# Chunked attention and a gated feed-forward block on one core: another order of all steps, with twelve warm-up products

## The chip, the core and the metric

The kernel runs on one NeuronCore of a Trainium2 chip. The metric is the time of one execution on the device in microseconds (us). It was measured three times before the change: 384.4, 385.7 and 385.95, median 385.7 us. A further execution was recorded by the profiler; all views and rows below are of that one.

## What is computed

Attention in chunks of 32 queries, each of which sees 8 memory keys and 56 neighbouring keys, for 4 batches, 8 heads, 768 positions and heads of 64; then a feed-forward block with a gate that mixes positions:

```
scores = q_chunk @ k_full.T / 8 ;  a = softmax(scores) ;  x = a @ v_full
h = gelu(x @ w_in) ;  u, v = halves of h            # w_in 512 x 1024
v_n = layernorm(v) * g_ln
gated = u * (w_sg @ v_n + b_sg)                      # w_sg 768 x 768
out = x + gated @ w_out                              # w_out 512 x 512
```

All of it is in f32. The large products are made in TensorE's rounded f32 type: each operand is split into a high and a low part, and a product is the sum of high-low, low-high and high-high.

## The kernel before, in words

The work is cut into named **steps**, each of which issues its instructions on one engine. A string `ORDER` (lines 36 to 95) lists all steps by name, and the last loop (lines 577 to 582) issues them in that order. The wrapper `InOrder` (lines 98 to 107) keeps each engine, and the queue of loads on SyncE (SP), in exactly this order; a step waits for the data and for the buffers it needs. A star behind a name picks the second engine that a step may use. So the order is written out by hand for five engines at once, and it is the only thing that says when a buffer is taken and given back.

**Attention** is done in 24 units u (4 batches of 6 blocks of 128 positions). `q`u, `k`u, `v`u are loads on SP (256, 368 and 512 KB). `S`u are the scores on TensorE: 32 small f32 products of two passes each, which makes 64 weight loads and 64 products. `mx`u, `sb`u (maximum and subtraction, VectorE), `ex`u (exponential, ScalarE), `sm`u, `sr`u (sum and reciprocal, VectorE), `nm`u (division, on VectorE, or on GpSimd with a star), `T`u (four transposes on TensorE, units 0 to 9), `p`u (copy from PSUM) and `A`u (attention times values, 64 small products, 64 weight loads) follow. `xc`u copies the result, `xh`u and `xl`u make its high and low part. There is one buffer for the scores, so S of the next unit waits for `sb`; one for A's result, so the next A waits for `xc`; one for the divided exponentials, so the next `nm` waits for `T`; and two each for q and k, so `q2` waits until S0 has run, `k4` until S2 has, and whatever stands behind a waiting load in the SP queue waits too.

**Weights** come as 64-bit floats and are converted on the chip. For each of eight 512 KB pieces of w_in (`ri10` to `ri13` for the half that makes v, `ri00` to `ri03` for the one that makes u) there are `d1` to `d4` (ScalarE and VectorE), `d5` (high part, ScalarE) and `d6` (low part, GpSimd, or VectorE with a star). `g..`, `ga..`, `gb..` load w_sg and split it, `ro.`, `d.o.` are w_out, `cb` and `cbh` load and halve g_ln and b_sg.

**Feed-forward.** `V`bt makes v of one block of 128 positions: 12 products of 512 columns. For the first three blocks of batch 0 it is made in two halves of 256 columns, `Va` with the pieces i10 and i11 and `Vb` with i12 and i13. `v1` to `v9` are gelu, layernorm and the split. `U`, `W` and `O` with three digits make u (12 products of 384 columns), the mixing over positions (18) and the output (12); `u.`, `w.`, `o1` stand behind them, and `out` stores.

A step `zz`n issues n **warm-up products** (line 573): the 128x128 identity times itself into a free PSUM buffer, read by nobody.

```
def warm(n):
    for _ in range(n if mms.free else 0):
        tensor.matmul(mms.free[0][:, 0:P], ident, ident, start=True, stop=True)

for name in ORDER.split():
    if name[0] == "z" and name[1] == "z":
        warm(int(name[2:]))
        continue
    does, eng = steps.pop(name.rstrip("*"))
    does(eng[name.endswith("*")])
```

Of the kernel before, what the change touches and what calls it, by code (L numbers as in the profile page):

```python
# [46 lines left out]
ex7 ga51 v303 T5 p5 sr6 nm6* v403 v503 S8 A5 T6 U000 ga20 v802 mx8 gb51 gb41 gb20 k9 ro0 g30 g01 ga01 xh5 v7
q10 q9 g31 v902* vx03 gb01 p6 xl5 v104 u1003 xc5 vy03 v603 sb8 v204 u2003 sm7 sr7 u1000 u2000 nm7 V05 ex8
u3003 ga31 v304 u4003 v703 v404 v803 S9 sm8 v504 vx04 sr8 mx9 v903 A6 T7 xc6 p7 v105 ga30 v205 u3000 g50 q11
k10 v8 k11 ga50 v305 sb9 u4000 vy04 gb31 gb30 v405 v505 gb50* vx05 nm8* v604 U012 U011 g00 S10 k12 A7 u1012  # L50
u2012 u3012 vy05 v605 mx10 v705 v704 T8 ex9 xc7 p8 U010 U013 v804 u4012 v904* v805 ga00 v905* sb10 A8 S11
d2o0* d3o0 gb00 d1o0 u1010 ro1 sm9 u1011 d4o0 u2011 ex10 xc8 u2010 u3010 u4010 u3011 u4011 d1o1 W003 d2o1 mx11
d3o1 w1003 sm10 d4o1 w2003 d5o1 w3003 d5o0 sr9 nm9* d6o1 ro2 q12 W000 W001 d1o2 d2o2* w1000 w4003* w1001 w2000
d3o2 w2001 sb11 W002 ro3 k13 q13 v11 v9 W011 T9 S12 k14 q14 w1002 w2002 d6o0* W010 w3001 d1o3 p9 d4o2 d2o3
d3o3 d4o3 sr10 d5o3 d6o3* w3000 w3002 u1013 W012 d5o2 mx12 nm10 sb12 w1010 yt10 w2010 ex12 w3010 ex11 w4001
w4000 d6o2 w4002 w1012 S13 mx13 z12 sm12 w2012 A9 z11 sm11 w1011 w2011 w3012 sr11 nm11 yt11 O000 O003 sb13
o1003 O001 u2013 u3013 sr12 o1001 v12 k15 v10 S14 O002 mx14 W013 nm12 ex13 w3011 xh6 xh8 w4012 sb14 u4013 xh7
xl8 V12 w1013 w2013 v112 w3013 o1002 o1000 ex14 w4013* Ed5 Ea5 k16 q15 Ec5 q16 Eb5 out003 S15 out001 out002
out000 k17 w4011* xl7 sm14 v212 yt12 sr14 sm13 V11 v312 sr13 v111 v211 v311 w4010 xl6 O011 U101 nm13* mx15
v411 sb15 v412 v512 yt13 vx12 xc9 A10 u1101 xc10 S16 vy12 v612 v511 A11 ex15 sm15 o1011 vx11 vy11 v611 v711*  # L60
nm14* v712 v812 v912* V10 mx16 U103 v110 v210 v310 u1103 U102 sr15 u2101 v410 sb16 ex16 sm16 u3101 sr16 u4101
v510 u1102 O012 v811 vx10 o1012 q17 S17 mx17 k18 q18 Ea6 Ec6 Eb6 Ed6 out011 O013 O010 u2102 xc11 u3102 xh9
v911 vy10 v610 yt14 o1013 nm15 sb17 u2103 xl9* A12 S18 V13 yt15 v710* v810 xh10 xh11 u4102 xl11 o1010 u3103
v113 xl10 v213 v313 v413 v14 out012 v13 out010 out013 k19 q19 q20 k20 V15 U110 u1110 v513 vx13 u4103 v910 mx18
nm16 sb18 vy13 v613 v713* U113 V14 xc12 v115 v215 v315 u2110 v813 ex17 u1113 v913 A13 S19 v114 v415 v515 vx15
u2113 u3113 v214 v314 v414 v514 vx14 u4113 vy15 z17 v615 v715* U100 U112 U111 u1100 v815 ex18 vy14 v614 v714
u3110 v814 u4110 u1111 v914* u2100 u2111 u3111 u4111 v915 W111 w1111 w2111 sm17 Ed7 W103 w1103 w2103 mx19 W101
w1101 sr17 w3111 w4111 xc13 w3103 u3100 v15 Eb7 Ec7 v16 Ea7 yt16 nm17* W100 A14 w2101 sb19 S20 w3101 u1112
xc14 u2112 u3112 ex19 u4100 w1100 w2100 A15 W102 W110 w1102 w2102 W113 w1110 w1113 w3100 w3102 w2110 w2113
yt17 w4103 W112 w4100 w4102 z18 w4101 w1112 w3110 w3113 O100 w4110* O103 sm18 sr18 u4112 w2112 w3112 o1103  # L70
o1100 O101 o1101 w4112* O102 xh12 xh13 w4113* O111 o1102 nm18 xl12* o1111 O110 sm19 V20 v120 v220 xh14 v320
mx20 sb20 v420 xl13 Ea8 q21 k21 Ed8 out101 Ec8 out103 out111 Eb8 k22 out100 out102 V21 v520 vx20 sr19 yt18
O113 O112 ex20 v121 xc15 vy20 v620 xl14 v221 nm19 A16 xc16 v321 o1110 v421 v521 v720* o1112 xh16 xh15 v820 S21
U202 U201 u1202 o1113 vx21 u2202 mx21 xl15 sb21 vy21 v621 V23 v920 yt19 u3202 v123 v223 u4202 xl16 v721* v323
u1201 v821 ex21 u2201 v423 v523 u3201 v921* vx23 U200 V22 v19 k23 out110 v17 out113 q22 A17 S22 Ec9 Ed9 q23
v18 out112 Eb9 Ea9 v122 xc17 xh17 vy23 v623 v723 v823 v923 v222 v322 xl17* u4201 V24 v422 v522 sm20 vx22 v124
v224 v324 sr20 v424 vy22 v622 V25 U203 v722 v822 v922 v524 u1200 u2200 u3200 u4200 u1203 u2203 v125 U213 v225
vx24 v325 v425 v525 vx25 mx22 U210 vy24 v624 u3203 u1213 u1210 nm20* sb22 v724 v824 U212 A18 xc18 sm21 u4203
u2213 u2210 vy25 S23 A19 U211 v625 u1212 u3213 u2212 sr21 v725 xc19 v825 u3212 u3210 v924 u4213 v925* u4212
yt20 mx23 nm21* yt21 Ea10 v20 Eb10 v21 Ed10 Ec10 W201 W212 w1201 u4210 w1212 w2201 w2212 W210 W200 sb23 w1200  # L80
w2200 w3201 w4201* w1210 w2210 W202 w3200 w3212 w3210 W203 w4210 ex23 ex22 sm22 z23 sr22 sm23 u1211 w1202 sr23
w1203 w2202 w3202 w4202* u2211 w4200 W213 w2203 w3203 w4203 nm22* u3211 u4211 yt22 W211 w1213 w2213 w1211 O203
o1203 O202 w2211 w3213 w3211 w4213 w4211* nm23* A20 O200 xc20 A21 O201 xh18 xh20 w4212* o1200 o1202 yt23 o1201
O213 O212 xh19 xl19 xl20 V31 v131 o1213 out202 out201 Ea11 out200 V32 v132 v232 v332 o1212 v231 v432 v532 Eb11
v22 Ed11 out203 O210 v23 Ec11 out212 v331 v431 xl18 U302 V30 O211 u1302 u2302 vx32 vy32 v632 v732 o1210 out210
v832 xc21 A22 u3302 xc22 v531 vx31 vy31 o1211 v631 v731 U301 xh22 u4302 v831 xh21 v932 v130 v230 A23 xl22 xl21
v931* v330 xc23 xh23 v430 v530 vx30 xl23 V34 V33 U303 v134 u1301 u2301 v234 u3301 v334 vy30 v630 v730 v434
v830 v930 u4301 u1303 v534 vx34 vy34 u2303 v634 v133 u3303 v233 v734 v333 v834 v433 v533 v934 vx33 u4303 V35
U312 v135 v235 v335 v435 v535 U310 u1310 u2310 vx35 u1312 u2312 vy33 v633 v733* v833 u3312 u4312 U313 u1313
u3310 vy35 v635 U311 U300 u4310 v735 v835 v933* v935* W310 u2313 u3313 u4313 W313 w1310 w2310 w1313 w2313 W301  # L90
w1301 w2301 w3301 W303 w1303 w2303 w3310 w3303 W312 W311 w3313 w1312 w2312 w4313* w4301 w1311 u1311 u1300
# [554 lines left out]
```

## Time and profile before

| | |
|---|---|
| median of three runs | 385.7 us (384.4 to 385.95) |
| the profiled execution | 383.29 us |
| its span, first to last instruction | 381.5 us |
| mean granted TensorE clock over the span | 0.998 |
| TensorE (PE) busy | 363.9 us, 95% |
| VectorE (DVE), ScalarE (ACT), GpSimd (POOL) busy | 65%, 41%, 34% |

The rows give, for each instruction or group, the start in us from the span's start, the length, the engine, the line of the code, the operation and the tiles that it writes and reads. PE is TensorE's products, PEld its weight loads. As every instruction is issued through one helper, all have line 106: the tiles tell them apart (`s` scores, `av` attention times values, `mma` to `mmd` the four PSUM buffers of all other products, `na` the divided exponentials, `pair` and `x` the attention's result, `raw`, `m`, `ex` the weights in conversion). An f32 product leaves two records. The column of the granted clock holds the level from the first recorded change on, so that it reads 1.00 also where none had been recorded yet.

### The profile page before, as it was taken

The page shows a single profiled execution, that of the slowest core. Times are in us where ns is not written, and L with a number is a line of the kernel's source. Part 1 is how long each engine was busy: PE and PEld are TensorE (multiplying, and loading weights), DVE is VectorE, ACT ScalarE, POOL GpSimd, SP SyncE. Part 2 cuts the span into 40 slices and gives each one's busy share as a digit, 9 for nine tenths or more (in the row PEclk, how much of TensorE's full clock was granted, in tenths as well). Part 3 has the DMA queues.
Part 4 walks back from the last instruction along what each step waited for, and adds up shares of the span by engine and source line. Part 5 has one row for each costly group of instructions (what it writes and reads, how often), then busy time and mean ns, then how long its engine had stood idle before and what let it go on. Part 6 is the DMA issues. An engine that isn't in the chain of part 4 may idle for free.

```text
span 381.5 us, 11092 instructions
## 1 busy us (share of the span) xinstructions
PE 363.9 (95%) x4788; PEld 340.7 (89%) x4788; DVE 247.5 (65%) x460; ACT 155.3 (41%) x296; POOL 131.3 (34%) x152
## 2 busy tenths in 40 slices
...
GB/s 242 350 316 308 309 181 212 225 66 171 207 173 163 159 74 211 130 95 74 4 11 140 117 217 14 144 10 140 25 3 54 189 50 2 3 0 2 0 63 147
DMA packets 24530, 47.66 MB, mean 125 GB/s; under 512 B 4384, under 2 KB 13600, under 8 KB 24480
## 3 DMA queue, kind: packets, MB, share of 16 engines
...
q8 instruction: 38, 0.62, 0.7%
q14 instruction: 12, 0.10, 0.1%
HBM read 36.96 MB, written 6.29 MB: 113 GB/s over the span
## 4 chain that ended last, share of the span: by engine, by line
PE 94%; DMA 3%; issue 1%; DVE 1%; SPq 0%; POOL 0%; POOLq 0%
PE mmd L106 23%; PE mmc L106 22%; PE mmb L106 19%; PE mma L106 17%; PE av L106 7%; PE s L106 5%; DMA qb<-in_qs 2%; DMA ka<-in_ks 1%; SPq L106 0%; POOL na L106 0%; DVE ea L106 0%; DVE mxa L106 0%; DVE xb L106 0%; POOLq L106 0%
## 5 line engine op out<-in xcount | busy, mean ns | idle before, releaser
L106 PE MATMUL s<-ka,qa 64*32 64x64 f32 x768 | 11.0, 238 | 6.2 <-DMA ka<-in_ks 4.2
L106 PEld LDWEIGHTS s<-ka,qa 64*32 64x32 f32 x768 | 8.9, 112 | 7.9 <-issue 5.1
L106 DVE SCALAR_TENSOR_TENSOR mmc<-mmc,g_half,b_half 128x384 f32<-128x384 f32 x10 | 6.2, 623 | 12.4 <-PE mmc L106 12.4
L106 DVE SCALAR_TENSOR_TENSOR mmd<-mmd,g_half,b_half 128x384 f32<-128x384 f32 x12 | 7.4, 620 | 10.2 <-PE mmd L106 10.2
L106 DVE SCALAR_TENSOR_TENSOR gb<-gb,mmb 128x512 f32<-128x512 f32 x10 | 6.9, 686 | 9.3 <-ACT gb L106 9.3
L106 PE MATMUL s<-kb,qb 64*32 64x64 f32 x768 | 11.0, 238 | 1.7 <-DVE ea L106 1.5
L106 ACT ACTIVATE ea<-ea 128x512 f32<-128x512 f32 x12 | 7.6, 635 | 11.0 <-DVE ea L106 11.0
L106 DVE STREAM_TRANSPOSE y<-na 128x512 f32<-128x512 f32 x14 | 9.8, 702 | 3.4 <-POOL na L106 1.7
L106 PEld LDWEIGHTS s<-kb,qb 64*32 64x32 f32 x768 | 8.9, 112 | 3.5 <-DVE ea L106 1.8
L106 PEld LDWEIGHTS av<-pt,va 64*64 64x64 f32 x512 | 9.3, 145 | 2.9 <-ACT pt L106 1.7
L106 PE MATMUL av<-pt,va 64*64 64x32 f32 x512 | 10.2, 230 | 1.3 <-ACT pt L106 1.3
L106 PE MATMUL mmc<-w_in_hi,paira 128*128 128x512 f32 (+1 forms) x40 | 9.5, 359 | 1.8 <-issue 1.8
L106 DVE TENSOR_REDUCE mxa<-s 128x8 f32<-128x512 f32 x8 | 5.4, 679 | 8.5 <-PE s L106 8.5
L106 PEld LDWEIGHTS av<-pt,vb 64*64 64x64 f32 x512 | 9.2, 145 | 1.9 <-issue 1.1
L106 POOL TENSOR_TENSOR na<-eb,rda 128x512 f32<-128x512 f32 x3 | 3.5, 1169 | 20.2 <-DVE rda L106 16.4
L106 DVE SCALAR_TENSOR_TENSOR ga<-ga,mmb 128x512 f32<-128x512 f32 x6 | 4.1, 681 | 9.8 <-ACT ga L106 9.8
L106 POOL TENSOR_TENSOR pairb<-uf,pairb 128x384 fp32r<-128x384 f32 x3 | 3.0, 1016 | 20.9 <-ACT pairb L106 20.9
L106 PE MATMUL av<-pt,vb 64*64 64x32 f32 x512 | 10.2, 230 | 0.0
L106 DVE SCALAR_TENSOR_TENSOR mmb<-mmb,g_half,b_half 128x384 f32<-128x384 f32 x6 | 3.7, 617 | 9.9 <-PE mmb L106 9.9
L106 POOL TENSOR_TENSOR paira<-uc,paira 128x384 fp32r<-128x384 f32 x3 | 3.1, 1047 | 20.1 <-ACT paira L106 20.1
L106 ACT ACTIVATE ga<-ga 128x512 f32<-128x512 f32 x12 | 7.6, 632 | 6.0 <-DVE ga L106 5.9
L106 PEld LDWEIGHTS av<-pt,vc 64*64 64x64 f32 x512 | 8.4, 135 | 1.8 <-issue 1.3
...
## 6 DMA issues: line engine op xcount, KB each, us to landing
...
va<-in_vs SPq DMA_DIRECT2D x8, 512.0 KB, 5.4
vb<-in_vs SPq DMA_DIRECT2D x8, 512.0 KB, 4.8
vc<-in_vs SPq DMA_DIRECT2D x8, 512.0 KB, 4.6
pt<-y SPq DMA_DIRECT2D x112, 32.0 KB, 1.9
...
```

Source lines behind the costliest of these rows:

```text
L106: return self.tc.keep_in_program_order(getattr(self.engine, name)(*args, **kw))
```

## The change

`ORDER` is replaced as a whole; nothing else is touched. The same steps stand in another order, some on their other engine, and the warm-up products become twelve instead of four: six ahead of S0, five between T1 and T2, one behind T4 (before: three ahead of S0 and one behind Vb02). The first lines of both strings, which hold the stretch that the prediction works out, and the last ones:

```
-zz1 q1 q0 k0 k1 ri11 ri10 zz2 S0 mx0 sb0 ex0 z0 sm0 sr0 q2 k2 S1 mx1 sb1 S2 d2i11* d2i10* ex1 d3i11 d3i10 sm1
-d1i10 d4i10 sr1 v0 ri13 k3 q3 ri12 v1 nm0* d5i10 T0 p0 nm1* A0 mx2 sb2 ex2 sm2 d1i11 d2i13* d1i13 d4i11 d3i13
-sr2 d4i13 d6i10 S3 T1 nm2* T2 xh0 d5i11 xl0 d6i11 xc0 d5i13 p1* A1 d2i12* d1i12 mx3 sb3 d3i12 d6i13* d4i12 xc1
-ex3 sm3 p2 xh1 xl1* v2 d5i12 d6i12* q5 ri00 d2i00* d1i00 ri01 Va00 A2 Vb00 d2i01* d1i01 d3i00 d4i00 d3i01 sr3
-d4i01 d5i00 v100 xh2 v200 v300 q4 ri02 k4 xl2 cb ri03 v3 k5 Va01 S4 q6 k6 g21 g41 g20 g40 g11 nm3* Vb01 T3
-d5i01 d2i02* xc2 v101 p3 d2i03* d1i02 Va02 v400 v500 mx4 vx00 d3i02 cbh v201 sb4 vy00 v600 v700 v800 v900
-d3i03 d4i02 A3 S5 Vb02 mx5 sb5 zz1 S6 ex4 xc3 xh3 sm4 xl3 V03 v301 v401 sr4 v501 d1i03 v102 v202 d4i03 d5i03
-d5i02 v302 ex5 d6i00* nm4 d6i02* d6i01 q7 g10 v6 v4 k7 v5 U001 T4 vx01 vy01 z5 v601 d6i03* ga40 gb40 v402 mx6
...
-out302 out303 out312 O301 o1301 out301 out213 O300 o1300 out300 O311 o1311 out311
+zz4 zz1 q0 q1 zz1 k0 k1 S0 mx0 sb0 ex0 z0 S1 sm0 sr0 nm0* ri12 ri13 mx1 sb1 T0 q2 k2 v0 q3 k3 ri10 d2i12*
+d2i13* d1i12 d1i13 d3i12 d3i13 d4i12 d4i13 p0 ex1 d5i12 d5i13 S2 mx2 sb2 ex2 d6i13 A0 xh0 d2i10* sm1 sr1 S3
+sm2 xl0 mx3 sr2 nm1* d6i12 T1 nm2* d3i10 sb3 k4 ri11 d1i10 p1 d4i10 d2i11* d1i11 d5i10 ri01 q4 ri00 d2i01* xc0
+v1 d3i11 d4i11 d5i11 ex3 zz1 zz4 T2 Vb00 S4 p2 d2i00* d1i01 d1i00 A1 xc1 xh1 v2 ri02 d2i02* k6 cb q5 k5 v3
+ri03 g40 g10 q6 g21 d6i11 d3i01 d6i10* sm3 sr3 nm3 d3i00 d4i01 d4i00 d5i01 T3 Va00 A2 v100 xl1 mx4 d3i02 sb4
+v200 Vb01 Va01 xh2 xl2 ex4 v300 v400 sm4 sr4 d5i00 d1i02 v101 xc2 p3 v500 v201 d4i02 d6i00* vx00 d6i01 cbh
+nm4* Vb02 S5 A3 T4 vy00 v600 mx5 sb5 v700 d1i03 xc3 d2i03* v301 zz1 v800 d3i03 d4i03 xh3 d5i02 ex5 p4 z5 v900*
+xl3* U001 Va02 S6 V03 d6i02 v401 v501 sm5 v102 v202 sr5 vx01 d5i03 d6i03 u1001 q7 ga21 v302 ga10 mx6 sb6 ex6
...
+out212 out311 out300 O312 O301 o1301 o1312 o1302 out312 O303 out301 out302 o1303 out303 O310 o1310 out310
```

TensorE's own steps up to the first full V product are, before: S0 S1 S2 T0 A0 S3 T1 T2 A1 Va00 A2 Vb00 Va01 S4 Vb01 T3 Va02 A3 S5 Vb02 zz1 S6 V03 (then U001 T4). After: S0 S1 T0 S2 A0 S3 T1 zz1 zz4 T2 Vb00 S4 A1 T3 Va00 A2 Vb01 Va01 Vb02 S5 A3 T4 zz1 U001 Va02 S6 V03.

## Rows read from the trace of the kernel before

**Rows 1.** The page of the profile, parts 1 and 4: busy time of the engines over the span, and the shares of the chain of work that ended last.
```profile
PE 363.9 (95%) x4788; PEld 340.7 (89%) x4788; DVE 247.5 (65%) x460; ACT 155.3 (41%) x296; POOL 131.3 (34%) x152
...
PE 94%; DMA 3%; issue 1%; DVE 1%; SPq 0%; POOL 0%; POOLq 0%
```

**Rows 2.** The view by windows, the first 40 us in stretches of ten: start and end, length, busy us (and instructions) of PE, PEld, DVE, ACT and POOL, the granted clock column, the share of the DMA engines in use and the GB/s that they moved.
```profile
0.00:10.00 10.00, 2.87 (x76) 2.36 (x80) 1.38 (x2) 1.35 (x2) 0.80 (x9) 1.00 0.70 245
...
10.00:20.00 10.00, 6.56 (x261) 5.48 (x262) 8.21 (x16) 6.99 (x13) 3.52 (x4) 1.00 0.97 358
...
20.00:30.00 10.00, 8.67 (x154) 7.61 (x155) 8.23 (x13) 7.27 (x14) 2.28 (x2) 1.00 0.86 285
...
30.00:40.00 10.00, 9.51 (x248) 8.93 (x247) 9.83 (x19) 8.98 (x18) 6.88 (x7) 1.00 0.96 331
```

**Rows 3.** The view of the waits, TensorE alone, over the whole span: who waited for whom, us in total, times, longest.
```profile
PE s L106 <- DMA ka<-in_ks: 4.2, 1, 4.2
...
PE mmc L106 <- issue: 1.8, 1, 1.8
```

**Rows 4.** The timeline of the first 30 us, TensorE's products alone: start, us, engine, line, operation, out<-in, shapes, count. In order: three warm-up products (two records each), the transpose step T2, the value step A1, four 256-column products of Va00, the value step A2, four 256-column products of Vb00.
```profile
1.42 1.65 PE L106 MATMUL mma<-ident 128*128 128x128 f32 x6 [1.42 <-POOL mhalf L106]
...
22.29 1.12 PE L106 MATMUL mmc<-ident,na 128*128 128x128 f32 x4 [1.33 <-POOL na L106]
...
23.33 1.93 PE L106 MATMUL av<-pt,vb 64*64 64x32 f32 x64
...
27.07 1.05 PE L106 MATMUL mmd<-w_in_hi,paira 128*128 128x256 f32 x4
...
28.05 1.20 PE L106 MATMUL av<-pt,vc 64*64 64x32 f32 x64
...
29.77 0.63 PE L106 MATMUL mmd<-w_in_lo,paira 128*128 128x256 f32 x4
```

**Rows 5.** The chain of work that ended last, in order of time (start, us, what, records): the first load of keys, S0, a half V product, a warm-up product, T4, a U product right behind a score step, a V product, an S step, an A step, a W product, an O product, and the addition behind the last O product.
```profile
1.62 5.51 DMA ka<-in_ks
...
7.28 1.19 PE s L106 x61
...
30.87 1.41 PE mma L106 x12
...
41.97 0.22 PE mmb L106 x2
...
48.08 0.44 PE mma L106 x4
...
52.45 2.30 PE mma L106 x12
...
54.75 2.78 PE mmd L106 x12
...
57.97 0.79 PE s L106 x53
...
58.76 1.06 PE av L106 x64
...
354.74 3.12 PE mmd L106 x18
...
371.39 2.08 PE mmd L106 x12
...
377.67 0.56 DVE xb L106
```

**Rows 6.** Instruction loading. First part 3 of the page, the row of the queue that brings instructions (packets, MB, share of 16 engines); then the DMA view of three short stretches, 14.3 to 14.4, 39.0 to 39.1 and 45.75 to 45.85 us, in each of which one packet of that queue began; then the timeline of TensorE from the value step A3 on (the idle time before a row and what ended it stand in brackets).
```profile
q8 instruction: 38, 0.62, 0.7%
...
q8 instruction: 1, 0.02, 58.8%
...
q8 instruction: 1, 0.02, 60.4%
...
q8 instruction: 1, 0.02, 67.2%
...
36.45 1.14 PE L106 MATMUL av<-pt,va 64*64 64x32 f32 x64
...
37.51 0.86 PE L106 MATMUL s<-kb,qb 64*32 64x64 f32 x64
...
38.87 0.63 PE L106 MATMUL mmc<-w_in_lo,paira 128*128 128x256 f32 x4
...
41.34 0.63 PE L106 MATMUL mmc<-w_in_hi,paira 128*128 128x256 f32 x4 [1.83 <-issue]
```

**Rows 7.** The timeline of the first 23 us, the other engines: the maximum of unit 0, GpSimd's division for unit 0, the maximum of unit 2, and a low part of a weight on GpSimd.
```profile
8.49 0.69 DVE L106 TENSOR_REDUCE mxa<-s 128x8 f32<-128x512 f32 x1 [8.49 <-PE s L106]
...
11.94 1.04 POOL L106 TENSOR_TENSOR na<-ea,rda 128x512 f32<-128x512 f32 x1 [1.12 <-DVE rda L106]
...
15.50 0.64 DVE L106 TENSOR_REDUCE mxc<-s 128x8 f32<-128x512 f32 x1
...
16.76 1.27 POOL L106 TENSOR_TENSOR w_in_lo<-ma,w_in_hi 128x512 fp32r<-128x512 f32 x1
```

**Rows 8.** The load of unit 1's values: its issue in the timeline, and its row in the DMA view of 12.65 to 13.2 us, whose last number is the us from issue to landing.
```profile
12.71 0.46 SPq L106 DMA_DIRECT2D vb<-in_vs  x1
...
vb<-in_vs SPq DMA_DIRECT2D x1, 512.0 KB, 8.4
```

More of the change, by code (lines that the diff above doesn't have):

```diff
@@ L42 @@
-d5i01 d2i02* xc2 v101 p3 d2i03* d1i02 Va02 v400 v500 mx4 vx00 d3i02 cbh v201 sb4 vy00 v600 v700 v800 v900
-d3i03 d4i02 A3 S5 Vb02 mx5 sb5 zz1 S6 ex4 xc3 xh3 sm4 xl3 V03 v301 v401 sr4 v501 d1i03 v102 v202 d4i03 d5i03
-d5i02 v302 ex5 d6i00* nm4 d6i02* d6i01 q7 g10 v6 v4 k7 v5 U001 T4 vx01 vy01 z5 v601 d6i03* ga40 gb40 v402 mx6
-sm5 v701 sb6 u1001 ga11 p4 ga21 ga10 U002 v801 A4 S7 U003 v502 u1002 sr5 u2002 vx02 u2001 ex6 xh4 u3001 xl4
-v901* xc4 v103 u3002 ga41 gb21 gb11 nm5* vy02 z6 v602 gb10 v702* u4001 mx7 sm6 sb7 V04 g51 k8 q8 u4002 v203
@@ L47 @@
[L47 to L91, printed above, removed]
@@ L92 @@
-w3312 u2311 u3311 u4311 w2311 w3311 W300 W302 w4311* w4303* w4312* u2300 u3300 w1300 u4300 w2300 w1302 w2302
-w3302 w4310 O312 o1312 O310 O313 w4302* w3300 w4300 O302 o1313 o1310 out310 out313 out211 O303 o1303 o1302
-out302 out303 out312 O301 o1301 out301 out213 O300 o1300 out300 O311 o1311 out311
+zz4 zz1 q0 q1 zz1 k0 k1 S0 mx0 sb0 ex0 z0 S1 sm0 sr0 nm0* ri12 ri13 mx1 sb1 T0 q2 k2 v0 q3 k3 ri10 d2i12*
+d2i13* d1i12 d1i13 d3i12 d3i13 d4i12 d4i13 p0 ex1 d5i12 d5i13 S2 mx2 sb2 ex2 d6i13 A0 xh0 d2i10* sm1 sr1 S3
@@ new lines @@
+xl3* U001 Va02 S6 V03 d6i02 v401 v501 sm5 v102 v202 sr5 vx01 d5i03 d6i03 u1001 q7 ga21 v302 ga10 mx6 sb6 ex6
+g20 k7 vy01 v601 nm5* u2001 v402 v4 ro0 v5 k8 A4 v701 u3001 ga20 xh4 v801 S7 T5 ga40 p5 z6 mx7 xl4 v502 vx02
+u4001 sm6 gb20 sr6 U002 sb7 v901 gb10 gb21 vy02 g11 xc4 ga11 u1002 v103 v203 u2002 v303 u3002 u4002 gb40* v403
+k9 v503 v602 v702 vx03 nm6* g01 q8 gb11 v6 g51 g31 q9 v7 g41 g30 V04 U003 A5 ex7 ga51 gb51* vy03 v603 S8 T6
+xh5 p6 ga01 ga41 v802 sm7 xl5 u1003 xc5 v703 mx8 u2003 gb01 sb8 sr7 u3003 v803 v902 U000 V05 v104 S9 A6 v903
@@ new lines @@
+gb41 u4003 v204 nm7* ex8 ga30 sm8 v105 sr8 v205 ga31 v304 v404 v305 v405 v505 g50 k10 q10 k11 q11 v8 v9 U012
+T7 mx9 u1000 v504 vx04 sb9 ga50 p7 xc6 gb50 u1012 u2000 u3000 d2o0* nm8* gb31 u4000 u2012 u3012 g00 U011 A7
+S10 vy04 v604 v704 vx05 mx10 u4012 vy05 v605 v705* gb30* sb10 U010 xc7 u1010 v804 T8 U013 p8* ga00 v805 v904*
+gb00* v905* d3o0 d1o0 u1011 u2010 u3010 u4010 ex9 A8 S11 u2011 mx11 u3011 u4011 d4o0 sm9 sr9 k12 ro1 W003
+d2o1* d1o1 ex10 w1003 w2003 w3003 d5o0 d3o1 W000 w1000 nm9 sb11 w2000 ex11 w3000 w4000 d4o1 d5o1 d6o1 z11
@@ new lines @@
+w4003 d6o0 W001 sm10 w1001 w2001 xc8 w3001 q12 ro2 d2o2* sr10 w4001* d3o2 k13 q13 d1o2 ro3 v11 W002 T9 w1002
+w2002 p9* w3002 S12 mx12 d4o2 nm10 sm11 d2o3* u1013 d1o3 d5o2 W012 sb12 d3o3 d4o3 d5o3 ex12 u2013 w1012 w2012
+yt10 W011 sr11 w1011 w2011 d6o3 d6o2* S13 nm11* w4002* A9 W010 u3013 w3011 k14 k15 q14 q15 O003 yt11 z12 sm12
+u4013 sr12 w4011* nm12 Ea5 mx13 sb13 o1003 O001 O000 O002 xh8 w3012 xh7 xh6 ex13 S14 o1000 W013 o1001 o1002
+xl6* xl7* w1010 mx14 w4012* sb14 Ed5 Ec5 Eb5 yt12 w2010 out003 v10 xl8 V12 v112 w3010 S15 V11 U101 q16 w1013
@@ new lines @@
+v12 k16 out002 out001 q17 k17 out000 v212 mx15 w4010* w2013 w3013 w4013 O011 ex14 v312 xc9 A10 sm13 sr13 v412
+v512 vx12 vy12 nm13 sb15 v111 ex15 xc10 S16 sm14 sr14 yt13 nm14* v612 o1011 A11 V10 u1101 v211 mx16 v712 v812
+v912* v311 sb16 v411 v110 xc11 v210 u2101 v310 v410 v510 v511 vx11 U102 O012 o1012 O013 O010 xh11 S17 vy11
+v611 xh10 vx10 o1013 sm15 sr15 v711 v811 vy10 v610 v710 xh9 U103 q18 Ed6 k18 Ec6 Ea6 Eb6 A12 mx17 yt14 nm15
+sb17 u1102 u2102 o1010 ex16 ex17 u3102 u1103 u2103 u3103 u3101 v810 yt15 S18 xl11 xl9 V13 xl10 v911 u4102 sm16
@@ new lines @@
+sr16 V15 nm16* u4101 mx18 v113 v213 v313 v910* sb18 k19 q19 v15 out011 v13 v14 out012 out013 out010 v413 v513
+vx13 vy13 v613 u4103 v713 ex18 v115 v813 v913 v215 v315 v415 v515 vx15 V14 U110 u1110 u2110 xc12 v114 v214
+v314 u3110 U113 u1113 A13 S19 v414 vy15 z17 v615 v715 v514 vx14 u2113 vy14 v815 xc13 u3113 u4113 mx19 U100
+u1100 u2100 v915 v614 U111 U112 v714 v814 u4110 sm17 v914* u1111 u3100 u4100 W100 w1100 Ed7 Ec7 Eb7 q20 v16
+Ea7 w2100 w3100 W101 yt16 sr17 nm17 sb19 u2111 u3111 u4111 W111 w1101 w2101 yt17 w1111 w2111 W103 k20 A14
@@ new lines @@
+w3111 xc14 w1103 w2103 w3103 w4103 S20 A15 W113 W102 u1112 u2112 u3112 w1113 w2113 w1102 mx20 w2102 W110 w1110
+w2110 W112 w1112 u4112 w4111 w4100 w3113 w3101 w4101 w3102 w4102 z18 sm18 w2112 O102 O100 O101 w3112 ex19
+w3110 O103 o1102 w4110 w4113* sr18 o1101 o1100 o1103 nm18* w4112 O110 sb20 o1110 O113 xh13 xl13 xh14 xh12 xl12
+V20 v120 v220 v320 ex20 O112 V21 Eb8 Ea8 Ec8 Ed8 yt18 v420 v520 sm19 out103 q21 vx20 v121 v221 sr19 xl14 o1113
+O111 vy20 v620 v720* out101 v17 out100 k21 k22 out102 v321 xc15 v421 S21 A16 xh15 v820 xl15 nm19 v521 U202 V23
@@ new lines @@
+v920* vx21 vy21 v621 xc16 u1202 v721 v821 xh16 v123 v921 o1111 o1112 u2202 v223 V22 U201 out113 v18 q22 out112
+k23 v19 mx21 u3202 u4202 v323 yt19 sm20 v423 v122 U200 v523 vx23 sr20 A17 vy23 xl16 v623 v723* v222 v322 sb21
+v422 u1200 u2200 u3200 ex21 v522 vx22 u1201 v823 xc17 S22 V24 xh17 v923* Eb9 out111 q23 Ec9 Ea9 v20 Ed9 out110
+U203 u4200 u2201 u3201 v124 v224 v324 vy22 v622 xl17 v722 mx22 v822 V25 v424 v922* v524 nm20* u1203 v125 u4201
+vx24 vy24 v225 v325 v624 v724* v425 U213 U210 v525 vx25 vy25 v625 v725* u2203 u3203 u1213 u2213 u1210 v824
```

15 lines of the change are left out of this document (added).

## The prediction, made before the changed kernel was run

> **What bounds the kernel now.** I read the page first: TensorE holds 95% of the span and 94% of the chain that ended last [rows 1]. Then the chain in order of time, for the price of each step at the high clock [rows 5]: S 0.79, A 1.06, T 0.44, half V 1.41, V 2.78, U and O 2.08, W 3.12 us, a warm-up product 0.22, and 0.22 more for a product right behind an S or an A (2.30 against 2.08). With the counts of the program (64 U and O, 32 W, 21 V and 6 halves, 24 S and A, 10 T, 23 such changes, one warm-up product behind S0) the work from S0 on is 353.9 us. S0 starts at 7.28, when its keys have landed, and the last product ends at 377.67 [rows 5]; so 16.5 us are lost. Where: by the end of Va00, at 28.05 [rows 4], the work done was worth 8.2 us of 20.8, which leaves 12.5; one wait of 1.83 inside Vb02 [rows 3, 6]; the rest is spread in tenths. So only the first 42 us can give anything: the other 336 us run without a wait of TensorE.
>
> Two things make up the 12.5. TensorE waits for a chain over the other engines. And it runs at the lower of its two clocks, 1.2 GHz: the column of the granted clock shows 1.00 here [rows 2], but durations don't. T2 took 1.12, A1 1.93, four 256-column products 1.05 at 27.07; then A2 took 1.20 and four such products 0.63 at 29.77 [rows 4]. The clock rose at about 28.1. TensorE had not been idle since 22.29 [rows 4], 5.8 us earlier.
>
> **The change, first stretch.** I walk the new order with these durations. Up to S1 nothing differs: k0 is the third load in both orders, S0 starts at 7.28, and the six warm-up products ahead of it (0.55 each at the low clock [rows 4]) end by 4.7, in time that is idle anyway [rows 3]; cost nothing. The division nm0 ends at 12.98 [rows 7]. T0 now goes before S2: 13.05 to 14.2, its copy p0 to 14.8; S2 14.2 to 15.4, so mx2 begins at 15.5, exactly as before [rows 7]. A0 can start at 15.4 instead of 16.66; I add 0.8 for an instruction packet (below), so it ends at 18.1, S3 at 19.3. T1 needs nm1 (ready 19.0): 19.3 to 20.4. Five warm-up products at 0.55: to 23.15. T2's input is ready at 21.6 (nm2 behind T1, 1.04 on GpSimd), so they delay it by 1.5 us; that is their price, up to 24.25 for the end of T2. Vb00 is then ready (low parts on GpSimd at 1.27 each [rows 7] done at 20.3, xl0 at 19.5).
>
> **When the clock rises** decides the next term. From T1 at 19.3 TensorE would not be idle again; with the 5.8 us of before the clock rises at 25.1. Bounds: 19 to 21, if the stretch from T0 to S3 already suffices, and 28.1, as before. I take 25.1, as it is the same interval in the same kind of work. The TensorE page of the Trainium skill (TensorE: Matmul & The Clock Gate, Part 1) speaks against such a search: the moment differs between runs of one kernel, and one should not fit to it. By that rule part of what a single profile shows here would not come back in the next run; one profile of before cannot show it.
>
> From there: Vb00 to 26.3, S4 27.1, A1 27.2 to 28.3, T3 28.75, Va00 30.3, A2 31.4, Vb01 33.0, Va01 34.4, Vb02 35.8, S5 36.6, A3 37.7, T4 38.15, one warm-up product, U001 40.4, Va02 41.85, S6 42.65, V03 45.6. The same set of steps was done before at the end of T4, 48.52 [rows 5]: a gain of **2.9 us**. What is left after it is the same set of steps in both, with 20 instead of 18 product-behind-S-or-A changes and no T behind an A instead of three (0.15 each): equal. The end is the same too: the last O, an addition of 0.56 [rows 5] and a store.
>
> **What must stay hidden for that.** Loads: v1 now stands behind ri11, ri01, q4 and ri00, and k4 holds SP from 12.6 until S2 has run. About 6.03 MB had moved by 20 us [rows 2]; v1 ends 7.39 MB in the new queue, so 1.36 MB more at 358 GB/s is 23.8, and 2.0 for the lag that the old v1 shows (5.70 MB, moved at 19.1, landed 21.1 [rows 8]): 25.8 against 27.2. At 285 GB/s [rows 2] it is 26.8, still in time. q5, k5 and v3 now wait behind k6 and so for S4 (27.1): v3 ends 1.93 MB later, at 331 GB/s [rows 2] 32.9 and the lag, 34.9 against 36.6. VectorE is busy 9.83 of 10 us between 30 and 40 [rows 2], and nm3 moves to it (0.69); in my walk its products come 0.6 to 1.5 us ahead of their use (xl1 30.8 for Vb01 at 31.4, xl2 32.9 for Vb02, d6i00 37.0 for U001, xl3 41.5 for V03 at 42.65). A slip there of 1 us is inside the range.
>
> **The instruction wait.** In 38 packets of 16 KB [rows 6] the 9576 loads and products [rows 1] come some 252 to a packet. Before, TensorE stood still for 1.83 us although nothing was awaited, in front of its 1462nd instruction (counted from the program: 128 for an S or A, 8 for a T, 24 for a half V), and went on 2.3 us after a packet had begun at 39.05 [rows 6]. A packet is thus asked for about 252 instructions ahead: at number 1209, in A3, 36.6 [rows 6], which makes 4.7 us from request to use. A3 and S5 hold 256 instructions and take under 2 us, so the packet came late. In the new order S5 and A3 are neighbours again: number 1209 is in Vb02 (34.9), number 1461 near the end of A3 (37.6). That is 2.7 us against 4.7: a wait of 2.0. At best the sequencer asks while it is still some products ahead of the array, and the wait is nothing. I take the middle, **1.0 us** back. For the same reason A0 gets its 0.8 (first packet at 14.3 to 14.4 [rows 6], plus 2.3, less the 15.9 at which its 452nd instruction is due). The Trainium skill's page on the launch (Runtime: NRT & Kernel Launch, Instruction fetch mechanics) calls the crossing of a packet mostly hidden; by it the term would be zero, which the 1.83 contradicts here at least once.
>
> **Sum.** -2.9 + 1.0 = -1.9 us. The profiled execution (383.29 for a span of 381.5) lies 2.4 below the median; I put the difference on the median: 385.7 - 1.9 = **383.8 us**. A measurement of this kernel can tell about 0.5% from no change, 1.9 us: the forecast lies on that bound.
>
> **Rivals.** (a) No instruction wait in A3 and none elsewhere: 385.7 - 2.9 = 382.8. For it: 37 of 38 packets cost nothing before. Against: S5 and A3 stand together again under loaded DMA engines. (b) An early rise of the clock, at 19 to 21: the warm-up products shrink to 0.22, T2 ends near 22.4, Vb00 to Va00 1.5 us sooner: 382.3, and 381.3 together with (a). Against: before, the stretch from 16.66 to 20.95 with one gap of 0.15 did not raise it. (c) The clock rises no earlier than before, at 28.1: Vb00 and S4 stay low, 1.0 us is lost: 384.8, no difference that can be told. (d) Slower: instruction packets bound the denser order. The packet of 45.8 came 4.4 us after the request at 41.34, so request to use can be 6.7. In the new order the packets at number 957 (in A1, 4.8 us after the one before) and 1461 (2.7) then wait 1.9 and 4.0: 5.9 lost against 2.9 won, 388.7. It turns into a loss from 5.2 us on ((5.2 - 4.8) + (5.2 - 2.7) = 2.9). Against: the only late packet measured took 4.7.
>
> **Chances and range.** Forecast 0.35 (half of it beyond the bound), (a) 0.20, (b) 0.12, (c) 0.20, (d) 0.13. Faster by over 0.5%: 0.17 + 0.20 + 0.10 = 0.47; within: 0.18 + 0.02 + 0.18 + 0.03 = 0.41; slower: 0.02 + 0.10 = 0.12. Range 381.3, (a) with (b), to 386.4, which leaves out the worse half of (d). The likeliest case's own range is 382.8 to 384.8.
>
> **What would show it.** S0 at 7.3, T0 near 13.1, T1 near 19.3, Vb00's first products near 24.3; the first A of about 1.1 instead of 1.93 tells when the clock rose (A1 by the forecast). A wait by nothing inside A3, 0 to 2 us, near 37. V03 ending near 46.6. After that no wait of TensorE above a few tenths. It is wrong if Vb00 starts after 25.5, if A1, A2 or A3 waits for a load, or if the steps behind V03 hold waits that sum to over 1 us.

## The result, and the profile of the changed kernel

| | before | changed |
|---|---|---|
| median of 21 runs of each | 384.42 us (382.25 to 388.9) | 388.0 us (383.72 to 390.68) |
| ratio of the times, 95% interval | | 1.0075 [1.0047, 1.0104] |
| the profiled execution, and its span | 383.29, 381.5 us | 386.5, 384.4 us |

The ratios, here and below, leave out slow runs, those more than 1.5% above the fastest of their kernel.

The change made the kernel slower. The prediction was 383.8 us in a range of 381.3 to 386.4: the sign is wrong and the range misses the median. It was counted from the 385.7 us of three runs; 21 runs put the kernel before at 384.42, and from there the forecast gain of 1.9 us leads to 382.5. In the two profiled executions the last product ends 3.4 us later than before (the addition behind it starts at 381.06 instead of 377.67 [rows 5]), so the profile holds most of the loss. It must be looked for twice: in the first stretch, which the prediction walked, and behind it, which the prediction put at nothing.

**The first stretch.** The view by windows, two stretches of ten us (columns as in [rows 2]):

```profile
0.00:10.00 10.00, 4.51 (x108) 4.00 (x109) 1.38 (x2) 1.71 (x2) 0.81 (x9) 1.00 0.75 247
...
20.00:30.00 10.00, 9.68 (x197) 9.24 (x199) 9.46 (x17) 8.95 (x16) 4.30 (x4) 1.00 1.01 343
```

In the first ten us the six warm-up products and an S0 0.37 earlier show (4.51 busy instead of 2.87 [rows 2]), in time that is idle otherwise. Between 20 and 30 us TensorE is busy 9.68 instead of 8.67 [rows 2] and does 197 instead of 154 products: there the new order wins. The timeline of its products in the same stretch, in the form of [rows 4]: S0, T0, A0, T1, five warm-up products, T2, the three parts of Vb00, A1, S5, A3 and the three parts of V03:

```profile
6.91 1.17 PE L106 MATMUL s<-ka,qa 64*32 64x64 f32 x64 [2.56 <-DMA ka<-in_ks]
...
12.67 1.12 PE L106 MATMUL mma<-ident,na 128*128 128x128 f32 x4 [1.90 <-POOL na L106]
...
15.94 1.93 PE L106 MATMUL av<-pt,va 64*64 64x32 f32 x64
...
19.49 1.11 PE L106 MATMUL mmb<-ident,na 128*128 128x128 f32 x4 [0.51 <-POOL na L106]
20.40 2.34 PE L106 MATMUL mmc<-ident 128*128 128x128 f32 x10
22.54 1.06 PE L106 MATMUL mmc<-ident,na 128*128 128x128 f32 x4
23.25 1.20 PE L106 MATMUL mmd<-w_in_hi,paira 128*128 128x256 f32 x4
24.24 0.76 PE L106 MATMUL mmd<-w_in_lo,paira 128*128 128x256 f32 x4
24.84 0.63 PE L106 MATMUL mmd<-w_in_hi,paira 128*128 128x256 f32 x4
...
26.57 1.14 PE L106 MATMUL av<-pt,vb 64*64 64x32 f32 x64 [0.32 <-ACT exe L106]
...
35.10 0.86 PE L106 MATMUL s<-kb,qb 64*32 64x64 f32 x64
36.92 1.14 PE L106 MATMUL av<-pt,va 64*64 64x32 f32 x64 [0.96 <-DMA va<-in_vs]
...
43.08 1.20 PE L106 MATMUL mmd<-w_in_hi,pairb 128*128 128x512 f32 x4
44.12 1.09 PE L106 MATMUL mmd<-w_in_lo,pairb 128*128 128x512 f32 x4
45.05 1.10 PE L106 MATMUL mmd<-w_in_hi,pairb 128*128 128x512 f32 x4
```

The length tells the clock: four 256-column products take 1.20, then 0.76, then 0.63, so it rose inside Vb00, near 24.5, and A1 takes 1.14 where it took 1.93 before [rows 4]. V03's successor starts at 46.08; the same set of steps ended at 48.52 before (T4 in [rows 5]). The first stretch gained 2.4 us in this execution. A3 did wait, not for instructions but for v3's load.

**Behind V03.** The view of the waits, TensorE alone (columns as in [rows 3]):

```profile
PE s L106 <- DMA ka<-in_ks: 3.5, 2, 2.6
PE mmb L106 <- DVE ua L106: 2.9, 1, 2.9
PE mma L106 <- POOL na L106: 1.9, 1, 1.9
PE av L106 <- ACT xa L106: 1.5, 1, 1.5
```

The second and the fourth row are new; they lie at 181 and 128 us, where TensorE had no wait before. The chain of work that ended last, near 120 us (start, us, what), shows the one at 128:

```profile
118.85 0.80 PE s L106 x53
...
120.06 0.69 SPq L106
...
120.79 6.80 DMA out<-xa
...
127.70 0.59 ACT xa L106
...
128.34 1.29 PE av L106 x63
```

SP's queue holds the two loads q17 and k17 ahead of out000, the store of a finished block. q17 is released by S15, which ends at 119.65; so the store is issued at 120.79, and it lands 6.8 us later (the two stores ahead of the loads, issued at 117.2 and 117.6, took 6.7 and 8.0). Only then may ScalarE write the same buffer (xc9), only then is A9's result out of `av`, and A10, which writes `av` next, stands for 1.53 us. The wait at 181 has a longer root. The changed kernel's SP queue, VectorE and TensorE there, three timelines one behind the other:

```profile
161.63 8.12 SPq L106 DMA_DIRECT2D pt<-y  x12
...
170.89 3.08 SPq L106 DMA_DIRECT2D pt<-y  x4
174.02 0.58 SPq L106 DMA_DIRECT2D ka<-in_ks  x1
...
177.13 0.71 DVE L106 STREAM_TRANSPOSE y<-na 128x512 f32<-128x512 f32 x1 [3.93 <-DMA ka<-in_ks]
...
179.30 0.55 DVE L106 SCALAR_TENSOR_TENSOR ua<-ua,mmb 128x384 f32<-128x384 f32 x1
180.43 0.55 DVE L106 SCALAR_TENSOR_TENSOR ua<-ua,mmb 128x384 f32<-128x384 f32 x1 [0.59 <-ACT ua L106]
...
181.04 0.44 PE L106 MATMUL mmb<-w_sg_hi,vha 128*128 128x384 f32 x1 [2.85 <-DVE ua L106]
...
183.70 0.52 PE L106 MATMUL mmb<-w_sg_lo,vhd 128*128 128x384 f32 x1
184.02 0.52 PE L106 MATMUL mmb<-w_sg_lo,vhe 128*128 128x384 f32 x1
...
185.14 0.33 PE L106 MATMUL mmb<-w_sg_hi,vhc 128*128 128x384 f32 x1
185.31 0.34 PE L106 MATMUL mmb<-w_sg_hi,vhd 128*128 128x384 f32 x1
```

From unit 10 on a transpose on VectorE (`yt`) and four groups of copies by DMA (`Ea` to `Ed`, for two units together) stand in the place of `T` and `p`. yt16 overwrites `y`, which the copies Ed7, Ec7, Eb7 and Ea7 read: sixteen DMAs that SP issues one by one from 161.6 to 174. The row names the load behind them as the releaser, but by the DMA view that load landed 3.3 us after 174.02, later than yt16 began; the copies are what `y` waits for. In the profile of e2 (below), which has the same order here, the row names them:

```profile
179.27 0.71 DVE L105 STREAM_TRANSPOSE y<-na 128x512 f32<-128x512 f32 x1 [3.29 <-DMA pt<-y]
```

The last four, issued from 170.9 to 173.4 behind two loads of 768 KB in all, take 3.5 to 5.4 us to land, the last one till near 176.9 (173.4 + 3.5). yt16 starts at 177.13 after VectorE has stood for 3.93 us, and behind it in the queue stand u2111 and u4111, which empty the PSUM buffer `mmb`. W103 needs that buffer: TensorE stands for 2.85 us. Before, VectorE came to the same yt16 only at 179.87, when those copies had landed, and it waited for nothing:

```profile
179.87 0.66 DVE L106 STREAM_TRANSPOSE y<-na 128x512 f32<-128x512 f32 x1
```

W103 itself then took 4.89 instead of 3.12 us [rows 5]: its products are 0.32 apart, and 0.17 only at its end. The windows of the changed kernel say why, in the column of the granted clock:

```profile
181.20:181.60 0.40, 0.40 (x3) 0.40 (x4) 0.37 (x2) 0.00 (x0) 0.00 (x0) 0.90 0.00 0
181.60:184.80 3.20, 3.20 (x12) 3.20 (x11) 2.20 (x4) 0.51 (x1) 0.00 (x0) 0.50 0.01 3
184.80:186.00 1.20, 1.20 (x11) 0.95 (x12) 0.00 (x0) 0.00 (x0) 0.00 (x0) 0.95 0.00 0
```

Just behind the idle 2.85 us the clock goes from 2.4 to 1.2 GHz for some 3.3 us, and in this execution the wait costs 1.8 us more.

The sum of the two profiles: -2.4 (first stretch) + 1.7 (A10, with its slower first products) + 3.0 (in front of W103, from where its first product was due) + 1.8 (in W103) = +4.1; the other steps, not followed one by one, make up the -0.7 to the +3.4 that the last product shows.

### The profile page after: what moved, and what is told of

The parts are those of the page before. It is cut to its first block, busy times and chain, and to the rows that moved or that the text cites. A ratio compares the mean times of both kernels' runs of the same rounds, so it can differ in the third digit from the quotient of the medians.

```text
span 384.4 us, 11113 instructions
## 1 busy us (share of the span) xinstructions
PE 366.5 (95%) x4804; PEld 343.6 (89%) x4804; DVE 249.6 (65%) x464; ACT 155.4 (40%) x297; POOL 122.3 (32%) x147
## 4 chain that ended last, share of the span: by engine, by line
PE 85%; DMA 8%; SPq 4%; DVE 2%; issue 1%; ACT 0%; POOL 0%; POOLq 0%; ACTq 0%; DVEq 0%
PE mmc L106 22%; PE mmd L106 21%; PE mma L106 17%; PE mmb L106 15%; PE av L106 6%; PE s L106 5%; DMA ka<-in_ks 4%; SPq L106 4%; DMA va<-in_vs 2%; DMA out<-xa 2%; POOL na L106 0%; DVE ua L106 0%; DVE rdb L106 0%; DVE y L106 0%; DVE na L106 0%
## 5 line engine op out<-in xcount | busy, mean ns | idle before, releaser
L106 DVE SCALAR_TENSOR_TENSOR mmc<-mmc,g_half,b_half 128x384 f32<-128x384 f32 x12 | 7.5, 621 | 20.1 <-PE mmc L106 20.1
L106 PE MATMUL mmd<-w_in_hi,paira 128*128 128x512 f32 (+1 forms) x48 | 12.1, 376 | 0.0
L106 POOL TENSOR_TENSOR paira<-ub,paira 128x384 fp32r<-128x384 f32 x3 | 3.1, 1025 | 26.2 <-ACT paira L106 26.1
L106 DVE SCALAR_TENSOR_TENSOR ga<-ga,mmd 128x512 f32<-128x512 f32 x10 | 6.9, 686 | 5.7 <-ACT ga L106 5.6
L106 DVE SCALAR_TENSOR_TENSOR gb<-gb,mmc 128x512 f32<-128x512 f32 x10 | 6.8, 684 | 5.7 <-ACT gb L106 5.7
L106 ACT ACTIVATE gb<-gb 128x512 f32<-128x512 f32 x12 | 7.6, 632 | 7.3 <-DVE gb L106 7.3
L106 DVE SCALAR_TENSOR_TENSOR mma<-mma,g_half,b_half 128x384 f32<-128x384 f32 x8 | 5.0, 621 | 7.8 <-PE mma L106 7.8
L106 PEld LDWEIGHTS mmd<-w_in_hi,paira 128*128 128x128 f32 x48 | 8.4, 200 | 1.2
L106 PE MATMUL mma<-paira,w_in_hi 128*128 128x384 f32 x48 | 9.3, 336 | 0.0
L106 POOL TENSOR_SCALAR rsb<-mvb 128x1 f32<-128x1 f32 x8 | 2.1, 264 | 22.3 <-DVE mvb L106 22.3
```

Of the source, the lines that this page charges most:

```text
L106: return self.tc.keep_in_program_order(getattr(self.engine, name)(*args, **kw))
```

## The experiments

My theory from this profile: the order behind V03 has two queue mistakes, worth some 6.5 us, and the first stretch is the gain that it was meant to be. The rival: the first stretch does not hold its gain from run to run. Each kernel below is an edit of the order alone; all its instructions are those of the changed kernel or, where it says so, of the one before, but for warm-up products left out or added in e6, e9, e10 and e11. Each was timed beside the kernel before, whose median was 383.9 to 384.5 us in the four groups of runs; the ratio is to that kernel in the same group.

**Each half alone.** e5 takes the order of before up to T4 and the changed one behind it; e4 the changed one up to V03 and that of before behind it.

> The order of the kernel before up to T4, and from there the remaining steps in the changed order: the other half of the change alone. Theory: the two waits (W103 behind yt16 with the fall of the clock, 4.8 us; A10 behind out000, 1.5) come from the order of the rest and are here too: 384.4 + 6 = 390, or 389 if VectorE meets them a little later. Rival (the loss comes from the first stretch, from late instruction packets and falls of the clock there): no slower than before by more than 1.5 us, 384 to 386.

> The changed order up to V03, and from there the remaining steps in the order of the kernel before. Theory: keeps the gain of the first stretch (V03 ends 2.4 us earlier than the same set of steps before, 3.2 with the tenths) and has none of the new waits: 381.2 to 382.2, a profiled span near 378.5. Rival (the first stretch only shifts work to VectorE and ScalarE, and the rest then waits whatever its order): waits of 2 us or more behind V03, no faster than before, 384 to 386. Rival (loss in the first stretch in other executions): 385 or more, with a late rise of the clock in the profile or in the runs' mean clocks.

e5: 389.77 us, ratio 1.0119 [1.0078, 1.016]. e4: 384.42 us, 1.0005 [0.9977, 1.0033]. So the part behind V03 loses about 5 us by itself, as the theory had it, and both new waits stand in e5's profile (1.4 and 2.8 us). But the first stretch alone gains nothing, against 2.4 us in the changed kernel's profile: here the rival is right. e4's profile shows where a gain goes, in A3:

```profile
35.98 1.02 PE L105 MATMUL av<-pt,va 64*64 64x32 f32 x56 [1.26 <-DMA va<-in_vs]
39.11 0.44 PE L105 MATMUL av<-pt,va 64*64 64x32 f32 x8 [2.12 <-issue]
39.48 1.12 PE L105 MATMUL mmd<-ident,na 128*128 128x128 f32 x4
```

A3 stops for 2.12 us after 56 of its 64 products although nothing is awaited, and the T step behind it takes 1.12 instead of 0.66: the clock has fallen.

**Each wait behind V03 alone, and both.**

```
e1:  W101 u2111 u3111 u4111 W111 w1101 w2101 yt16 sr17 nm17 sb19 yt17   (was: W101 yt16 sr17 nm17 sb19 u2111 ...)
e2:  out002 out001 out000 q17 k17 v212                                  (was: out002 out001 q17 k17 out000 v212)
e3:  both
```

> The changed order with one move: yt16, sr17, nm17 and sb19 stand behind u2111, u4111, w1101 and w2101 on VectorE instead of ahead of them. Theory: VectorE stood in yt16 until 177.1 for the transfers of E7, and the freeing of a PSUM buffer (u4111) waited behind it; that cost TensorE 3.0 us at W103 and, as its clock then fell for 3.4 us, another 1.8. Both go: about 4.8 us faster than the changed kernel (median 388.0 to about 383.2, its profiled span 384.4 to 379.6), no wait at W103 and no lower clock there. Rival (the wait moves on): the next PSUM buffer or S20 waits instead and under 1 us is gained, 387 or more. Rival (the loss lies in the first stretch, where other executions differ from the profiled one): this wait is in the profile alone, and the median stays at 386 to 388.

> The changed order with one move: the store out000 is issued ahead of the loads q17 and k17 instead of behind them. Theory: q17 waits for S15, so the store left at 120.8 and landed at 127.6, and xc9, which overwrites its buffer, held A10 by 1.5 us. Issued at about 118 it lands by 125: 1.5 to 1.7 us faster than the changed kernel, 386.4, and no wait at A10. Rival (the wait moves on): S17 or another A waits for the loads that are now later, no difference. Rival (loss in the first stretch): no difference in the median, whatever A10 does.

> The changed order with both moves (yt16 and its three steps later, out000 ahead of q17 and k17). Theory: 6.4 us faster than the changed kernel, 381.6 and a profiled span of 378; faster than the kernel before (384.4) by 2.8, which is what the first stretch gains. Rival (the wait moves on): under 2 us faster than the changed kernel, 386 or more. Rival (loss in the first stretch): 385 to 387.

e1: 384.13 us, 0.9985 [0.9954, 1.0016]; W103 waits no more: 3.9 us less than the changed kernel's 388.0. e2: 387.48, 1.0063 [1.0034, 1.0093]; A10 waits no more, but the median is only 0.5 lower, as is e3's against e1's: the 1.7 us that the changed kernel's profile shows for the store are not shown by the medians. e3: 383.67, 0.9968 [0.9936, 1.0001]: 4.3 lower than the changed kernel, so the two moves take back its loss against the kernel before, most of it by e1's, but the -2.4 of the first stretch is not there (388.0 - 6.4 would be 381.6). The profiles of e1, e2 and e3 have stops by nothing that the changed kernel's had not. e1, inside the five warm-up products, e2, inside A1, then e3, inside A3 with the step behind it, then e3's granted clock:

```profile
23.90 0.56 PE L105 MATMUL mmc<-ident 128*128 128x128 f32 x1 [2.28 <-issue]
```

```profile
26.27 0.90 PE L105 MATMUL av<-pt,vb 64*64 64x32 f32 x46
29.61 0.85 PE L105 MATMUL av<-pt,vb 64*64 64x32 f32 x18 [2.45 <-issue]
```

```profile
35.77 1.02 PE L105 MATMUL av<-pt,va 64*64 64x32 f32 x56
39.76 0.44 PE L105 MATMUL av<-pt,va 64*64 64x32 f32 x8 [2.96 <-issue]
40.12 1.12 PE L105 MATMUL mmd<-ident,na 128*128 128x128 f32 x4
```

```profile
39.00:42.50 3.50, 2.74 (x18) 2.68 (x18) 1.03 (x2) 2.25 (x5) 0.00 (x0) 0.50 0.94 344
42.50:46.00 3.50, 3.50 (x15) 3.50 (x14) 3.44 (x6) 1.97 (x4) 1.43 (x2) 0.56 0.53 200
```

e3 stops for 2.96 us and then runs some 6 us at the lower clock: V03 ends at 50.7 instead of 46.1, so one stop takes back twice what the first stretch had won. The order up to there is the same in the changed kernel and in e1, e2 and e3; only the execution differs. Counted in TensorE's program, weight loads and products together, e1's stop is behind number 698, e2's behind 952, e3's behind 1460. e4's, and that of before [rows 6], come at the same 1460.

**Does the stop belong to the step or to the number?** e6 is e3 without the five warm-up products (20 instructions) ahead of T2; e9 is the kernel before with these five put between T1 and T2.

> The order with both moves (383.7), without the five warm-up products between T1 and T2. Theory (they raise the clock sooner): T2 begins about 1 us sooner, near 21.7, but the clock rises later, up to 28 as in the kernel before, and S4, A1 and Va00 run low, 1 to 2 us: the sum is 0.5 to 1 slower, 384.4. Rival (the products ahead of them keep TensorE busy enough): the clock rises no later and the kernel is 1 us faster, 382.7.

> The kernel before with five warm-up products between T1 and T2 and nothing else changed. Theory: T2 is delayed by 1.4 us (from 22.3 to 23.7), TensorE is busy from 18.7 on and the clock rises some 3 us sooner, so A1 and Va00 run at the high clock (0.9 and 1.4 us less): 0.8 faster than before, 383.6. Rival (warm-up products do not bring the clock sooner): only the delay is left, 385.8.

e6: 383.52 us, 0.9978 [0.9946, 1.0009]: neither of the two expectations, and no difference to e3 that can be told. e9: 385.61, 1.0032 [0.9999, 1.0066]: the five products bring nothing, though the clock rose at 24.05 instead of 28.1. e9's profile has two stops, in A2 and in S5:

```profile
27.21 1.00 PE L105 MATMUL av<-pt,vc 64*64 64x32 f32 x52
30.14 0.42 PE L105 MATMUL av<-pt,vc 64*64 64x32 f32 x12 [1.93 <-issue]
...
40.34 0.84 PE L105 MATMUL s<-kb,qb 64*32 64x64 f32 x62
42.13 0.27 PE L105 MATMUL s<-kb,qb 64*32 64x64 f32 x2 [0.94 <-issue]
```

They stand behind numbers 952 and 1460 again, and in e6 the stop (2.78 us) has moved from A3 into T4, where number 1460 now lies. It belongs to the number, and what stops is whatever step stands across it. That a packet of instructions is what is awaited there, the DMA views show. The 13 profiles hold 20 stops by nothing of 0.2 us or more, and each time TensorE goes on 2.2 to 2.6 us after a packet of the instruction queue has begun. For e3's stop this is the packet between 37.2 and 37.3, for a restart at 39.76:

```profile
q8 instruction: 1, 0.02, 68.7%
```

Behind A2's stop in e9 the clock fell again (0.52 from 31.0 to 34.4), and what the earlier rise had won was gone.

**Orders that leave the packet more time.** e8 is e3 with Va02 right behind Vb02, so that 24 long products stand ahead of S5 and A3. e10 is e8 without any warm-up product. e7 is e3 with v3's load issued right behind ri02, ahead of k6, cb, q5 and k5. e11 is e10 with that load.

```
e8:   nm4* Vb02 Va02 S5 A3 T4 ... xl3* U001 S6      (was: nm4* Vb02 S5 A3 T4 ... xl3* U001 Va02 S6)
e10:  e8, and: q0 q1 k0 k1 S0 ... ex3 T2            (was: zz4 zz1 q0 q1 zz1 k0 k1 S0 ... ex3 zz1 zz4 T2; the last zz1 too)
e7:   v2 ri02 v3 d2i02* k6 cb q5 k5 ri03            (was: v2 ri02 d2i02* k6 cb q5 k5 v3 ri03)
```

> The order with both moves, and Va02 right behind Vb02 instead of behind U001, so that 1.4 us of products stand ahead of S5 and A3. Theory (the packet of instructions that begins near number 1461 is asked for near 1209 and takes over 4 us): the time between the two grows from 2.7 to 3.6 or more, the wait by nothing inside A3 (3.0 us in the profile of the order with both moves) falls below 1.5, the load of v3 is in time, and the clock does not fall behind it: 1 to 2 us faster, 382.2. Rival (the loads of k5 and v3 and not the packet): the same wait inside A3, no difference, 383.7.

> The order with both moves and Va02 ahead of S5 (382.75), without any of the twelve warm-up products. Theory (they are worth nothing in sum: T2 starts sooner by what a later rise of the clock costs): 382.3 to 383.3. Rival (they raise the clock sooner and that pays): 384 or more, with the clock rising 3 us later in the profile. A wait for instructions, if there is one, stands 48 instructions earlier in the steps, again in front of number 1461 of the program.

> The order with both moves (383.67), and the load v3 issued right behind ri02, ahead of k6, cb, q5 and k5. Theory: v3 is no longer what A3 waits for, but the instruction packet is due at the same place and takes its turn, or k5, which is now later, holds S5: no difference, 383.2 to 384.2, and a wait by nothing inside A3 of 1 us or more in the profile. Rival (the loads bound this stretch): A3 starts 1 us sooner and 1 us is gained, 382.7.

> The changed kernel with both moves behind V03 (yt16 behind u2111 u4111; out000 ahead of q17 k17), Va02 right behind Vb02, no warm-up product at all, and v3's load issued right behind ri02, ahead of k6 cb q5 k5. My theory is that the gains of the separate edits (no queue waits behind V03; a short stop by nothing in A3; no stop for v3) add up: about 381.3 to 382.0 us against 384.4 for the kernel before, ratio about 0.992, faster than both kernels. Rival: v3's earlier load only helps where A3 would wait for it, and with Va02 between Vb02 and A3 it no longer does: then it is 382.4, as without the early load. Another rival: with A3 free to start sooner, the stop by nothing at TensorE's instruction number 1461 less the warm-ups grows to 2 us or more and the clock falls behind it: 383.5 or more.

| | median, us (lowest to highest) | ratio to before | stop by nothing in S5, A3 or T4 | V03 ends |
|---|---|---|---|---|
| e3 | 383.67 (380.04 to 386.46) | 0.9968 [0.9936, 1.0001] | 2.96 | 50.7 |
| e8 | 382.75 (380.92 to 385.77) | 0.9967 [0.9936, 0.9997] | 0.47 | 47.0 |
| e10 | 382.39 (381.09 to 383.81) | 0.9944 [0.9913, 0.9974] | 0.31 | 47.3 |
| e7 | 382.5 (379.31 to 385.67) | 0.9938 [0.9893, 0.9983] | 0.64 | 47.2 |
| e11 | 382.72 (380.79 to 385.83) | 0.9968 [0.9935, 1.0] | none | 46.4 |

The intervals of these five overlap, so their order among themselves is not settled; e7 and e10 are faster than the kernel before by their intervals, e8 just so, and e7 and e10 beat the changed kernel by 5.5 and 5.6 us. e10's median lies where it was expected, e8's 0.55 above; e7's lies at its rival's 382.7, and its stop is shorter than the 1 us expected. e10 was to show what the twelve warm-up products are worth: nothing that can be seen. Without them its clock rose at 25.15, and its runs lie closest together. e11's profile is the best of all, with a span of 379.3 us and this wait by nothing, from the view of TensorE's waits:

```profile
PE mmd L105 <- issue: 2.0, 1, 2.0
```

The stop by nothing that is left stands in front of Va00, behind number 952 (in e10 too, 1.80 us there); behind number 1460, which now lies in T4, there is none, and the clock doesn't fall. Its median does not follow its profile: 382.72, where I had expected 381.3 to 382.0; it agrees with the rival, that v3's early load gains nothing once Va02 stands ahead of A3, though its interval doesn't exclude a gain.

**Why one profile misled.** Each run also lists its mean granted clock. For the 21 runs of the changed kernel it has a median of 0.991, and 0.996 in the profiled one; for the kernel before 0.998 to 0.999 in the four groups; for e10 and e11 0.999. A mean 0.005 lower is 384 x 0.005 / 0.5 = 3.8 us more at half speed, which costs up to 1.9 us: about the 1.5 us by which the changed kernel's median lies above its profiled run. That the missing clock is the fall behind the stops and behind W103's wait is what the profiles of e1, e2, e3, e4, e6, e9 and the changed kernel show one by one; for the runs that only have a mean it is not shown, since a run whose clock rises early and falls again (e4's profile: up at 5.0, down at 8.4, up at 22.1 us) has a lower mean too. The changed kernel's fastest run, 383.72, has a mean of 0.980, and e7, one of the fastest orders, a median of 0.994: the mean alone doesn't tell how long an execution took.

## Why the prediction was wrong

**The step that failed** is the sentence "What is left after it is the same set of steps in both ... equal". The same set of steps is the same work, but not the same queues. The diff replaces the order to its end, and the walk stopped at V03. Two places in the rest put an instruction that waits for a DMA ahead of one that TensorE needs: out000 behind q17 and k17 on SP (1.7 us), and yt16 ahead of u2111 and u4111 on VectorE (3.0 us, and 1.8 for the clock that falls behind it). That is 6.5 us of this profile costed at 0. e5 finds the loss with the rest alone, e1 takes 3.9 of it back with one move, e3 4.3 with both. How much of the 6.5 an execution loses differs: W103 was waited for in e2 and e5 too (2.22 and 2.81 us), but the clock didn't fall behind it there, and the store's 1.7 is not seen in the medians. The text had named it among the things that would make it wrong ("if the steps behind V03 hold waits that sum to over 1 us"), but gave it no place in the sum, the rivals or the range.

**The instruction wait** was right in kind and wrong in size, and the forecast gain of 1.9 us hung on it: the first stretch alone gains nothing (e4, 1.0005 [0.9977, 1.0033]). The wait was put at 1.0 us between 0 and 2.0, in A3. It was hidden in the changed kernel's profile, where A3 waits for v3's load (the packet began at 34.7, and A3 reached number 1460 only near 37.9). In A3 it was 0.35 us in e1, 0.21 in e2, 2.96 in e3 and 2.12 in e4; e1 and e2 stood for 2.28 and 2.45 at another number instead. What the term left out is the fall of the clock behind it: V03 ended at 50.7 in e3, 4.6 us later than in the changed kernel, with a stop of 2.96. Rival (d) had this mechanism and both numbers, 957 in A1 and 1461 in A3, as the places (952 and 1460 by the stops, 254 apart where it had taken 252); e2 and e3 stop there, but for long at one of them only. That its 388.7 is near the median is luck: the changed kernel's profile has neither stop, and most of the loss goes with e1's move.

**The Trainium skill** (Runtime: NRT & Kernel Launch, Instruction fetch mechanics) calls the crossing of a packet mostly hidden. 37 of 38 packets in the kernel before agree; the 1.93 us of e9 and the 2.96 us of e3 do not, and there the short instructions of score and value steps make up 232 and 240 of the 254 ahead of the number. The Trainium skill's page on TensorE (TensorE: Matmul & The Clock Gate, Part 1), which warns against fitting to the moment of the rise, is borne out: the first rise came between 5.0 us (e4, where S0 took 0.85 instead of 1.17) and 28.1 us (the kernel before), and the five products that were put in for it bring nothing (e6, e9).

**What held:** S0 (predicted 7.3, measured 6.91), T0 (13.05, 12.67), T1 (19.3, 19.49), Vb00 (24.25, 23.25), the rise of the clock (25.1, near 24.5), A1's length, V03's end (46.6, 46.1). The last is in part luck: 0.96 for v3's load stands where 1.0 for instructions was put. v1 was in time; v3 was not: issued at 28.64, landed 8.1 us later, 36.8 against the 34.9 worked out, a wait of 0.96 where none was expected. The lag of 2.0 us, read from one load, was too little here.
